# Local attention, top-2 MoE and GLU on one core: three experts begin on the first two batches, the router takes two batches at once, v is loaded once

## The chip, the core and the metric

The kernel runs on one core of one Trainium2 chip. The metric is the device time of one execution in microseconds; lower is better. The engines are TensorE (PE, with its weight load PEld), VectorE (DVE), ScalarE (ACT), GpSimd (POOL) and SyncE (SP). SP issues most transfers from memory, POOL the indirect ones.

## The reference

Three blocks follow one another; all is computed from float32 values.

```python
# attention: q, k, v are [4 batches, 8 heads, 576, 64]
mask_plain = (rel >= 0) & (rel < 32)                      # heads 0 to 3
mask_dil = (rel >= 0) & (rel < 128) & (rel % 4 == 0)      # heads 4 to 7
attn = softmax(where(mask, q @ k.T / 8, -1e9)) @ v
x = attn.transpose(0, 2, 1, 3).reshape(2304, 512)
# mixture of experts: 8 experts of 512 x 1024 x 512, two per row
noisy = x @ w_gate + log1p(exp(x @ w_noise)) * noise
top2 = two largest of noisy; weights = softmax over the two
out[row] += weight * (relu(x[row] @ w1[e]) @ w2[e])       # for both experts of a row
# gated linear unit, 512 x 1536 x 512
out = (silu(x @ w_gate2) * (x @ w_val)) @ w_out
```

## The kernel before

Every engine runs its instructions in the order in which the program writes them, so the place of a line in the Python loops is its place in the engine's queue. Waits between engines are found from the data.

**Attention** has 36 units: a batch has 9, of two blocks of 64 queries each (plain heads, one mixed unit, dilated heads). Because masks are local, a block needs 96 keys. Loop step i does the scores of unit i+1 (`at_S`, L194 puts in the mask, L201 the product), its maximum (DVE), then for unit i−1 the product with v (`at_AV`) and the norm (DVE, which sends the rows to the table `zd` in memory), for unit i−2 the transposes into `xTb`, and for unit i the transposes of the probabilities. v of a batch and head type is a tile of 96 partitions x 4 heads x 9 blocks x 65; neighbouring blocks share 32 rows, which memory holds twice.

**The router** is a generator, `routing`: logits, top two, the row's rank within its expert, and from that a slot number. Products of one-hot matrices (`ob` for the place within 128, `oa` for the column) turn slot numbers into the index table `inva`. It runs in four passes (`groups`, 4 or 5 blocks of 128 rows each, one per batch); three lie in attention, started at i = 11, 20 and 29, and the last in the MoE. `go(n)` and `pump_on(n)` in other code take n pieces of the generator, so each piece is a DVE instruction between those of the host code.

**The MoE** gives an expert up to 640 rows (CAP). A segment is an expert with a range of its slots, and has 8 steps (one per 128 columns of the hidden layer): load 512 KB of weights (`load_raw`, five steps ahead), split them (`split`: high part `whi` on ACT, remainder `wlo` on DVE, L173 and L175; two steps ahead), the hidden layer `moe_h` (three products per chunk, L657), relu into high part and remainder (`hhi` on ACT, `hlo` on DVE, L669 and L670), the output product `moe_y` of the step before (L696). Rows of x are gathered by POOL (`gather_x`, L591) during the segment before, turned (on PE, or in DVE's 32 x 32 transposes, L603, for the segments in DVE_SEGS) and split (`parts`, L616 and L618). Segments: experts 0 and 1 start with slots 0 to 255, which the first two batches fill; then their slots 256 to 639; experts 2 to 6 whole; expert 7 in two parts: 88 steps, of which 0 to 15 are 256 wide, 16 to 31 are 384, 32 to 71 are 640.

**The conversion of the GLU weights** rides on MoE steps named in the list CVS: `cv_tick` takes apart 8-byte numbers with three ACT and seven DVE instructions (L783 to L791) on 512 KB, behind the step's other DVE work. The seven instructions of a load come three ticks later. From step 32 on, five steps in six have a tick.

**The GLU** (72 steps, L1046 and L1070) runs on PE to the end.

`late_consts` casts constants that come with `ccon`. The part under `tc.If` is for experts with over 640 rows, which these inputs do not have.

Of the kernel before, what the change touches and what calls it, by code (L numbers as in the profile page):

```python
# [25 lines left out]
CAP = 640  # L26
EARLY = 256
# [13 lines left out]
def attn_moe_glu_kernel(ctx, tc, qT, kT, vB, cst, wgn, noise, wm, wz, out):  # L41
# [33 lines left out]
    idx = keep.tile([128, NA * E], I32, name="idx")  # L75
# [12 lines left out]
    def load_qkv(b, t):  # L88
# [34 lines left out]
    zs = gp.tile([128, N], F32, name="zs")  # L123
# [12 lines left out]
    V.tensor_copy(maskb.rearrange("p a k -> p (a k)"), zs[:, 0:C_END - C_MASK])  # L136
# [32 lines left out]
    def split(i, eng=V):  # L169
# [125 lines left out]
    groups = [(0, 4), (4, 9), (9, 13), (13, 18)]  # L295
    base = gp.tile([128, 5, E], F32, name="base")
    V.memset(base[:, 0, :], 0.0)
    inva = gp.tile([128, NA * E], F32, name="inva")
    idx0 = gp.tile([128, 2, 2], I32, name="idx0")
# [9 lines left out]
    def routing(gi):  # L309
        g0, g1 = groups[gi]  # L310
        n = g1 - g0
# [6 lines left out]
        def s_z(q):  # L318
            z = bank("f")
            for c in range(4):  # L320
                T.matmul(z[c * 32:c * 32 + 32, 0:S // 2], lhsT=wg[:, c, :],
                         rhs=xTb[gi][:, c, q * (S // 2):(q + 1) * (S // 2)], start=True, stop=True,
                         skip_group_check=True)
            o = gi * S + q * (S // 2)
            A.activation(zs[:, o:o + S // 2], z[:, 0:S // 2], AF.Copy)
# [65 lines left out]
        def s_slot():  # L391
            R = X["f"][:, 128:128 + n * E].rearrange("p (g e) -> p g e", g=n)
            tot = X["f"][:, 176:176 + E]
# [5 lines left out]
            if gi == 1:  # L399
                V.tensor_tensor(base[:, 2, :], base[:, 2, :], floor0, op=OP.max)  # L400
# [8 lines left out]
            a1 = tl("a1", [128, 2, n])  # L409
# [4 lines left out]
            ca = tl("ca", [128, 2, n])  # L414
            V.scalar_tensor_tensor(ca, a1, 8.0, X["ii"], op0=OP.mult, op1=OP.add)
            yield
            sb = tl("sb", [128, 2, n])
# [3 lines left out]
        def s_rows():  # L421
            rf = tl("rf", [128, 2, n])
            V.scalar_tensor_tensor(rf, X["ca"], 128.0, X["sb"], op0=OP.mult, op1=OP.add)
            yield
            V.tensor_scalar(rf, rf, 64.0 * 128 + N, None, op0=OP.add)
            yield
            V.tensor_copy(rowi[:, :, g0:g1], rf)
            yield
            ov = tl("ov", [128, n])
            V.tensor_tensor(ov, X["a1"][:, 0, :], X["a1"][:, 1, :], op=OP.max)  # L430
            yield
            V.tensor_scalar(ov, ov, float(CAP // 128), None, op0=OP.is_ge)
# [12 lines left out]
            V.reciprocal(ww[:, 0, g0:g1], sm)
            yield
            V.tensor_tensor(ww[:, 1, g0:g1], X["ex"], ww[:, 0, g0:g1], op=OP.mult)
            yield
            no = tl("no", [128, n])
            V.tensor_scalar(no, ov, -1.0, 1.0, op0=OP.mult, op1=OP.add)  # L450
            yield
            for k in range(2):
                V.tensor_tensor(wm_[:, k, g0:g1], ww[:, k, g0:g1], no, op=OP.mult)
                yield
            V.tensor_tensor(wm_[:, 0, g0:g1], wm_[:, 0, g0:g1], ov, op=OP.add)
            yield

        def onehots(eng, pairs):
            if "ob" not in X:
                tl("ob", [128, 2 * n, 128], F16)  # L460
                tl("oa", [128, 2 * n, NA * E], F16)
            for i, k in pairs:
                eng.tensor_scalar(X["ob"][:, 2 * i + k, :], iotb, X["sb"][:, k, i:i + 1], None,
                                  op0=OP.is_equal)
                yield
                eng.tensor_scalar(X["oa"][:, 2 * i + k, :], iotc, X["ca"][:, k, i:i + 1],
                                  tokid[:, g0 + i:g0 + i + 1], op0=OP.is_equal, op1=OP.mult)
                yield

        pool = [(i, 1) for i in range(n - 2, n)]  # L470
        mine = [(i, k) for i in range(n) for k in range(2) if (i, k) not in pool]
        order = mine + pool

        def s_inv(pairs):
            iv = X["f"][:, 256:256 + NA * E]
            for pr in pairs:
                j = 2 * pr[0] + pr[1]
                T.matmul(iv, lhsT=X["ob"][:, j, :], rhs=X["oa"][:, j, :], start=pr == order[0],
                         stop=pr == order[-1], skip_group_check=True)

        def s_acc():
            iv = X["f"][:, 256:256 + NA * E]
            if gi == 0:
                V.tensor_copy(inva, iv)
                yield
# [3 lines left out]
            if gi == 1:  # L489
                V.tensor_scalar(idx0, inva.rearrange("p (a e) -> p a e", e=E)[:, 0:2, 0:2], float(ID0), None,  # L490
                                op0=OP.add)
                yield
            if gi == 3:
# [3 lines left out]
                V.tensor_reduce(mx, base[:, 4, :], axis=AX, op=OP.max)  # L497
# [5 lines left out]

        LAG = 1 if gi < 3 else 0
        s_z(0)
        yield NEXT
        s_z(1)
        yield NEXT
# [8 lines left out]
        for _ in onehots(G, pool):  # L517
            pass
        h = len(mine) // 2
        yield from onehots(V, mine[:h])  # L520
        yield NEXT
        A.activation(X["ex"], X["ex"], AF.Exp)
        for _ in range(LAG):
            yield
        s_inv(mine[:h])
        yield from onehots(V, mine[h:])
        yield NEXT
        for _ in range(LAG):
            yield
        s_inv(mine[h:] + pool)  # L530
        yield from s_acc()
        if gi == 3:
            yield NEXT
        yield from s_rows()
        if gi == 3:
            V.tensor_copy(row0, rowm[:, :, 0:LOW // 128])
            yield
            V.tensor_copy(w0, wm_[:, :, 0:LOW // 128])
            yield NEXT
            o = X["f"][:, 0:4 * NSLOT].rearrange("p (t k) -> p t k", t=4)  # L540
            regroup(o, inva[:, 0:NSLOT])
            V.tensor_scalar(idx4, o, 4.0, ccon[:, C_PART + 1:C_PART + 2], op0=OP.mult, op1=OP.add)
            yield NEXT
            o = X["f"][:, 160:160 + 16 * NT].rearrange("p (t k) -> p t k", t=4)
            regroup(o, rw.rearrange("p a k t -> p (a k t)"))
            o4 = o.rearrange("p t (a k) -> p t a k", a=2)
            V.tensor_scalar(row4.rearrange("p t k n -> p t (k n)"), o4[:, :, 0, :], 4.0,
                            ccon[:, C_PART:C_PART + 1], op0=OP.mult, op1=OP.add)
            yield
# [639 lines left out]
```

## Time and profile before

| | |
|---|---|
| median of 3 runs | 1062.88 us (1056.6 to 1073.88) |
| profiled execution | 1065.96 us, span 1063.9 us |
| mean granted clock of TensorE in it | 0.984 of full speed |
| attention | 0 to 113.4 us |
| MoE, 16 steps of 256 | 113.4 to 177.2 us |
| MoE, 16 steps of 384 | 177.2 to 252.9 us |
| MoE, 40 steps of 640 | 252.9 to 531.8 us |
| MoE, expert 7 (8 of 384, 8 of 256) | 531.8 to 595.2 us |
| GLU | 595.2 to 1063.9 us |
| busy | PE 1024.8 us (96%), DVE 600.0 (56%), ACT 427.2 (40%), POOL 331.5 (31%) |

The profile shows one execution. Times in rows are microseconds from the span's start. PE's share of busy time is a mean over stages with different limits, so the stages are looked at one by one.

### The profile page before, as it was taken

How to read it: one execution, taken by the hardware profiler on the slowest of the kernel's cores; microseconds unless marked ns; L12 is line 12 of the kernel's file. 1: busy time of each engine (PE TensorE's matmuls, PEld its weight loads, DVE VectorE, ACT ScalarE, POOL GpSimd, SP SyncE). 2: the span in 40 equal slices, each digit the busy share in tenths (PEclk: the TensorE clock that was granted, in tenths of full speed). 3: DMA queues.
4: the chain of work that ended last, by engine and by line, in shares of the span. 5: the costliest groups of instructions: out<-in, count | busy, mean ns of one | idle time of the engine just before them, and what ended most of it. 6: DMA issues, size and time to landing. Idle time of an engine off the chain costs nothing. (4 is left out here: it accounts for less than half of the span.)

```text
span 1063.9 us, 16850 instructions
## 1 busy us (share of the span) xinstructions
PE 1024.8 (96%) x6561; PEld 920.1 (86%) x6562; DVE 600.0 (56%) x1259; ACT 427.2 (40%) x840; POOL 331.5 (31%) x324
## 2 busy tenths in 40 slices
PE   8988988899999999999999999799999999999998
PEld 5776777788999989899989899699999999999997
DVE  3587685468898788897865443134244233343222
ACT  4786543355565555565544322123122122122111
POOL 0023347626343526260001477315126035000000
PEclk8998999999999999999999999899999999999999
DMA  9994355566677777867686586101101101000000
GB/s 252 260 281 148 105 162 179 198 201 187 243 266 254 240 238 242 285 221 238 219 294 223 209 299 228 58 10 40 40 13 43 35 20 40 30 1 1 30 1 30
DMA packets 60980, 161.33 MB, mean 152 GB/s; under 512 B 10048, under 2 KB 17344, under 8 KB 60224
## 3 DMA queue, kind: packets, MB, share of 16 engines
q1 hardware_dynamic: 47904, 120.95, 35.4%
q0 software_dynamic: 12560, 38.82, 11.1%
q8 instruction: 52, 0.85, 0.3%
q10 hardware_dynamic: 432, 0.44, 0.1%
q14 instruction: 32, 0.26, 0.1%
HBM read 121.37 MB, written 38.80 MB: 151 GB/s over the span
## 5 line engine op out<-in xcount | busy, mean ns | idle before, releaser
L591 POOL DMA_INDIRECT xg<-zd,idx x139 | 158.0, 1137 | 168.4 <-DVE xtl L618 127.3
L591 POOL DMA_INDIRECT yg<-zd,row x126 | 122.8, 974 | 200.4 <-DVE yg L844 128.3
L657 PE MATMUL bA<-xth,whi 128*128 128x320 f32 (+2 forms) x452 | 115.9, 314 | 11.9 <-DVE hlo L670 6.1
L657 PE MATMUL bA<-xtl,whi 128*128 128x320 f32 (+2 forms) x452 | 114.9, 312 | 0.2 <-issue 0.2
L657 PE MATMUL bA<-xth,wlo 128*128 128x320 f32 (+2 forms) x452 | 114.6, 311 | 0.0
L1054 DVE TENSOR_TENSOR t<-bB,ex 128x384 f32<-128x384 f32 x36 | 20.1, 558 | 152.6 <-ACT ex L1052 137.8
L669 ACT ACTIVATE hhi<-bA 128x640 fp32r<-128x640 f32 (+2 forms) x73 | 42.4, 581 | 155.7 <-PE bA L657 129.2
L175 DVE TENSOR_TENSOR wlo<-raw,whi 128x1024 fp32r<-128x1024 f32 x80 | 97.2, 1215 | 8.9 <-ACT whi L173 7.7
L657 PEld LDWEIGHTS bA<-xth,whi 128*128 128x128 f32 x452 | 80.6, 190 | 20.8 <-DVE hlo L670 9.2
L173 ACT ACTIVATE whi<-raw 128x1024 fp32r<-128x1024 f32 x88 | 92.7, 1054 | 0.0
L670 DVE SCALAR_TENSOR_TENSOR hlo<-bA,hhi 128x640 fp32r<-128x640 f32 (+2 forms) x73 | 48.9, 669 | 74.8 <-ACT hhi L669 59.1
L657 PEld LDWEIGHTS bA<-xtl,whi 128*128 128x128 f32 x452 | 79.3, 190 | 1.4 <-issue 0.5
L657 PEld LDWEIGHTS bA<-xth,wlo 128*128 128x128 f32 x452 | 79.5, 190 | 0.0
L1052 ACT ACTIVATE ex<-bB 128x384 f32<-128x384 f32 x36 | 17.7, 492 | 151.7 <-PE bB L1046 120.5
L1058 ACT ACTIVATE th<-t 128x384 fp32r<-128x384 f32 x72 | 37.9, 526 | 87.7 <-DVE t L1055 71.8
L1054 DVE TENSOR_TENSOR t<-bA,ex 128x384 f32<-128x384 f32 x36 | 20.1, 558 | 93.3 <-ACT ex L1052 82.3
L1059 DVE TENSOR_TENSOR tl<-t,th 128x384 fp32r<-128x384 f32 x72 | 40.3, 559 | 42.7 <-ACT th L1058 40.9
L1046 PE MATMUL bA<-x2h,wl 128*128 128x384 f32 x288 | 57.7, 340 | 4.6 <-issue 4.6
L1046 PE MATMUL bB<-x2h,wh 128*128 128x384 f32 x288 | 57.3, 341 | 0.0
L1046 PE MATMUL bA<-x2h,wh 128*128 128x384 f32 x288 | 56.5, 338 | 0.3 <-PEq L977 0.3
L1046 PE MATMUL bB<-x2h,wl 128*128 128x384 f32 x288 | 56.4, 337 | 0.0
L1046 PE MATMUL bB<-x2l,wh 128*128 128x384 f32 x288 | 56.3, 337 | 0.0
(233 smaller groups left out, 2353.3 us busy)
## 6 DMA issues: line engine op xcount, KB each, us to landing
raw<-in_wm SPq DMA_DIRECT2D x88, 512.0 KB
r<-in_wz SPq DMA_DIRECT2D x36, 512.0 KB
zd<-y SPq DMA_DIRECT2D x40, 256.0 KB
whd<-cvh SPq DMA_DIRECT2D x36, 256.0 KB
wld<-cvl SPq DMA_DIRECT2D x36, 256.0 KB
wh<-whd POOLq DMA_DIRECT2D x12, 768.0 KB
wl<-wld POOLq DMA_DIRECT2D x12, 768.0 KB
v<-in_vB SPq DMA_DIRECT2D x7, 877.5 KB
```

The lines of the kernel that those rows point to most:

```text
L173: A.activation(whi[i], raw[i], AF.Copy)
L175: eng.tensor_tensor(wlo[i], raw[i], whi[i].bitcast(F32), op=OP.subtract)
L591: G.indirect_dma_start(out=g, out_offset=None, in_=src, in_offset=bass.IndirectOffsetOnAxis(ap=ix, axis=0))
L657: T.matmul(hp[:, q, 0:cw], lhsT=wt[:, ws], rhs=xt[:, c, q * cw:q * cw + cw], start=c == 0 and j == 0, stop=c == 3 and j == 2)
L669: A.activation(a3, hp, AF.Relu)
L670: V.scalar_tensor_tensor(l3, hp, 0.0, a3.bitcast(F32), op0=OP.max, op1=OP.subtract)
L1046: T.matmul(p[:, q, 0:LOW], lhsT=w[:, ws], rhs=x[:, c, :], start=c == 0 and j == 0, stop=c == 3 and j == 2, skip_group_check=True)
L1052: A.activation(ex, p[:, 0, 0:LOW], AF.Sigmoid)
L1054: V.tensor_tensor(t, p[:, 0, 0:LOW], ex, op=OP.mult)
L1058: A.activation(a, t, AF.Copy)
L1059: V.tensor_tensor(l, t, a.bitcast(F32), op=OP.subtract)
```

## The change

Three experts (NE) start with slots 0 to 255 instead of two, so the segments are experts 0, 1, 2 with 256, then the same three with 384, then experts 3 to 6 with 640 and expert 7 in two parts: 96 steps, of which 0 to 23 are 256 wide, 24 to 47 are 384, 48 to 79 are 640. Expert 2's weights are loaded and split twice. The router has two passes of nine blocks: batches 0 and 1 in attention from i = 20, batches 2 and 3 in the MoE, a few instructions per step. Its one-hots are built by wide two-input instructions on DVE. POOL keeps the gathers and loses the splits, its one-hots and the spreading copies `xk` (now on ACT). v is loaded once, on partitions 32 to 95; partitions 0 to 31 are copied from 64 to 95 by DVE. CVS starts eight steps later. Of the early splits, two are left in attention. Loads of constants and early weights move.

```diff
+NE = 3
-            SP.dma_start(v[:, :, a:z, :], vB[b, t, :, :, a:z, :])
+            SP.dma_start(v[32:96, :, a:z, :], vB[b, t, :, :, a:z, :])
+    def before_v(b, t, a, z):
+        v = vt[b, t]
+        if a == 0:
+            V.memset(v[0:32, :, 0, :], 0.0)
+            a = 1
+        V.tensor_copy(v[0:32, :, a:z, :], v[64:96, :, a - 1:z - 1, :])
...
-    segs = [(0, 0, EARLY), (1, 0, EARLY), (0, EARLY, CAP), (1, EARLY, CAP)] \
-        + [(e, 0, CAP) for e in range(2, E - 1)] + [(E - 1, 0, LOW), (E - 1, LOW, CAP)]
+    segs = [(e, 0, EARLY) for e in range(NE)] + [(e, EARLY, CAP) for e in range(NE)] \
+        + [(e, 0, CAP) for e in range(NE, E - 1)] + [(E - 1, 0, LOW), (E - 1, LOW, CAP)]
...
-            eng.tensor_tensor(wlo[i], raw[i], whi[i].bitcast(F32), op=OP.subtract)
+            V.tensor_tensor(wlo[i], raw[i], whi[i].bitcast(F32), op=OP.subtract)
...
-    groups = [(0, 4), (4, 9), (9, 13), (13, 18)]
...
+    def logits_of(b, banks):
+        for q, bk in enumerate(banks):
+            z = bank(bk)
...
+    def routing(gi, banks):
+        n = NT // 2
+        g0, g1 = gi * n, gi * n + n
...
-                eng.tensor_scalar(X["ob"][:, 2 * i + k, :], iotb, X["sb"][:, k, i:i + 1], None,
-                                  op0=OP.is_equal)
-                yield
-                eng.tensor_scalar(X["oa"][:, 2 * i + k, :], iotc, X["ca"][:, k, i:i + 1],
-                                  tokid[:, g0 + i:g0 + i + 1], op0=OP.is_equal, op1=OP.mult)
...
+            for k in range(2):
+                for i in range(0, n, 3):
+                    V.tensor_tensor(ob[:, k, i:i + 3], iotb[:, None, :].to_broadcast([128, 3, 128]),
+                                    sb[:, k, i:i + 3, None].to_broadcast([128, 3, 128]), op=OP.is_equal)
+                    yield
+                    if gi == 0:
+                        yield
+                        yield
+                V.tensor_tensor(oa[:, k], iotc[:, None, :].to_broadcast([128, n, NSLOT]),
+                                ca[:, k, :, None].to_broadcast([128, n, NSLOT]), op=OP.is_equal)
+                yield
+                V.tensor_tensor(oa[:, k], oa[:, k], tokid[:, g0:g1, None].to_broadcast([128, n, NSLOT]),
+                                op=OP.mult)
...
-            if s < 2:
+            if s < NE:
                 gather(g, xd[0:2 * S, :], idx0[:, a, e:e + 1])
...
-            G.tensor_copy(spread(g), by_chunk(rows))
+            A.activation(spread(g), by_chunk(rows), AF.Copy)
...
-    DVE_SEGS = (3, 11)
-    CVS = [17, 20, 23, 26, 29] + [32 + round(1.2 * j) for j in range(3 * NK + CV_LAST - 4)]
+    DVE_SEGS = (NE + 1, len(segs))
+    CVS = [25, 28, 31, 34, 37] + [40 + round(1.2 * j) for j in range(3 * NK + CV_LAST - 4)]
...
         if i > 2:
-            pump_on(3)
+            pump_on(1)
         moe_relu(i)
-        go(5)
+        go(2)
...
-        sp = split(i + 2, G if i < 11 and i % 2 else V) if i >= 2 else iter(())
+        sp = split(i + 2)
...
-    LOADS = (15, 17, 19, 23, 25)
-    SPLITS = (20, 22, 24, 26)
+    LOADS = (15, 17, 28, 33, 34)
+    SPLITS = (21, 23), (31, 33)
+    halves = [split(j) for j in range(2)]
...
-        if i == 2:
+        if i == 7:
             SP.dma_start(ccon[:, 128:C_MASK], cst[:, 128:C_MASK])
...
-            if (i - 11) % 9 == 0:
-                route.append([routing((i - 11) // 9), False])
+            if i in (11, 30):
+                route.append([logits_of((i - 11) // 9, "ff"), False])
+            elif i == 20:
+                route.append([routing(0, "ff"), False])
...
+        if i == 0:
+            before_v(0, 0, 0, 2)
+        elif i == 1:
+            before_v(0, 0, 2, NB)
+            V.tensor_copy(maskf[:, 192:], zs[:, 192:C_END - C_MASK])
+        elif i < NU and i % 9 in (0, 4):
+            before_v(i // 9, i % 9 // 4, 0, NB)
...
-        if i == 6:
+        if i == 12:
             late_consts()
...
-    route.append([routing(3), True])
+    route.append([routing(1, "fe"), True])
```

DVE in the last segment of 384 rows, before (steps 27 to 29, L670 is `hlo`, L603 and L618 the transpose and remainder of gathered rows, L175 the remainder of the weights, L783 to L791 the conversion of GLU weights):

```order
L670 SCALAR_TENSOR_TENSOR hlo<-bB,hhi 128x384
L603 STREAM_TRANSPOSE xg<-xg 128x512
L175 TENSOR_TENSOR wlo<-raw,whi 128x1024
L618 TENSOR_TENSOR xtl<-xg,xth 128x4x128
L670 SCALAR_TENSOR_TENSOR hlo<-bA,hhi 128x384
L603 STREAM_TRANSPOSE xg<-xg 128x512
L175 TENSOR_TENSOR wlo<-raw,whi 128x1024
L618 TENSOR_TENSOR xtl<-xg,xth 128x4x128
L670 SCALAR_TENSOR_TENSOR hlo<-bB,hhi 128x384
```

The same place now (steps 44 and 45, also the last segment of 384 rows; hlo is L675, the transpose L608, wlo L189, xtl L623, the conversion L788 to L796):

```order
L675 SCALAR_TENSOR_TENSOR hlo<-bA,hhi 128x384
L608 STREAM_TRANSPOSE xg<-xg 128x512
L189 TENSOR_TENSOR wlo<-raw,whi 128x1024
L623 TENSOR_TENSOR xtl<-xg,xth 128x4x128
L788 TENSOR_TENSOR cvw<-r,cvw 128x512
L790 TENSOR_SCALAR cvc<-cvw 128x512
L791 TENSOR_SCALAR cvh<-cvw 128x512
L793 SCALAR_TENSOR_TENSOR cvc<-r,cvc 128x512
L794 SCALAR_TENSOR_TENSOR cvh<-cvw,cvh 128x512
L795 TENSOR_SCALAR cvl<-cvh 128x512
L796 SCALAR_TENSOR_TENSOR cvl<-cvc,cvl 128x512
L675 SCALAR_TENSOR_TENSOR hlo<-bB,hhi 128x384
```

In these eight steps before, two had the seven conversion instructions; now seven have them.

POOL's queue before, from its first work in attention to the first MoE segments (L463 and L466 are one-hots, L643 spreads gathered rows):

```order
L463 TENSOR_SCALAR g_ob<-iotb,g_sb 128x128
L466 TENSOR_SCALAR g_oa<-iotc,g_ca,ccon 128x144
L463 TENSOR_SCALAR g_ob<-iotb,g_sb 128x128
L466 TENSOR_SCALAR g_oa<-iotc,g_ca,ccon 128x144
L175 TENSOR_TENSOR wlo<-raw,whi 128x1024 x3
...
L175 TENSOR_TENSOR wlo<-raw,whi 128x1024
L591 DMA xg<-zd,idx_140 128x512 x2
L643 COPY xk<-xg 128x512 x2
```

POOL's queue now, from the same place to the last gather of x:

```order
L596 DMA xg<-zd,idx_145 128x512 x6
L596 DMA xg<-zd,idx 128x512 x3
L596 DMA xg<-zd,idx_86 128x128 x124
```

Only gathers are left of POOL's work before the GLU's loads.

DVE in attention now, where one unit has the one-hots and another also the work in v (L444 compares three blocks at once, L450 and L453 make `oa` of nine, L120 and L122 are `before_v`, L223 the maximum, L287 the norm):

```order
L223 TENSOR_REDUCE nm<-bA 128x4
L450 TENSOR_TENSOR g_oa<-iotc,ca 128x360
L453 TENSOR_TENSOR g_oa<-g_oa,ccon 128x360
...
L444 TENSOR_TENSOR g_ob<-iotb,sb 128x384
L287 TENSOR_TENSOR xs<-bd,rec 128x256
L444 TENSOR_TENSOR g_ob<-iotb,sb 128x384
L120 MEMSET v 32x4x65
L122 COPY v<-v 32x4x520
L223 TENSOR_REDUCE nm<-bB 128x4
```

Before, DVE had two instructions per block and choice there, 128 and 144 wide, and nothing of v.

## Rows read from the trace of the kernel before

**Rows 1.** Busy time by stretch: start:end, length, each engine's us, clock, DMA.

```profile
0.00:113.40 113.40, 100.18 (x1545) 74.97 (x1547) 75.95 (x319) 75.52 (x241) 18.91 (x20) 0.92 0.77 223
113.40:177.20 63.80, 56.06 (x416) 48.39 (x415) 45.20 (x142) 27.76 (x56) 33.94 (x31) 1.00 0.53 167
177.20:252.90 75.70, 70.98 (x333) 62.69 (x334) 45.84 (x66) 35.64 (x53) 39.83 (x37) 0.95 0.60 196
252.90:531.80 278.90, 277.25 (x1556) 251.81 (x1555) 234.75 (x368) 152.20 (x217) 102.78 (x88) 1.00 0.72 239
```

**Rows 2.** Timeline of PE, first products of attention units: start, duration, instruction.

```profile
26.45 0.33 PE L194 MATMUL bB<-maskb,identb 128*128 128x192 bf16 x2
...
28.63 0.33 PE L194 MATMUL bA<-maskb,identb 128*128 128x192 bf16 x2
...
76.64 0.33 PE L194 MATMUL bA<-maskb,identb 128*128 128x192 bf16 x2
...
99.04 0.33 PE L194 MATMUL bB<-maskb,identb 128*128 128x192 bf16 x2
```

**Rows 3.** Timeline of PE, first products of neighbouring MoE steps, 384 and 256 wide.

```profile
236.19 0.33 PE L657 MATMUL bA<-xth,whi 128*128 128x384 f32 x1
...
240.38 0.33 PE L657 MATMUL bB<-xth,whi 128*128 128x384 f32 x1
...
579.48 0.28 PE L657 MATMUL bA<-xth,whi 128*128 128x256 f32 x1
...
582.30 0.28 PE L657 MATMUL bB<-xth,whi 128*128 128x256 f32 x1
```

**Rows 4.** The page's DMA issues: queue, count, KB of each.

```profile
v<-in_vB SPq DMA_DIRECT2D x7, 877.5 KB
```

**Rows 5.** Timelines of PE and DVE in attention; brackets hold the idle time before.

```profile
17.77 0.91 PE L201 MATMUL bA<-k,q 64*64 64x96 f32 x14 [2.14 <-DMA k<-in_kT]
...
31.80 0.23 DVE L145 CAST trib<-ccon 128x128 bf16<-128x128 f32 x1 [2.89 <-DMA ccon<-in_cst]
...
32.22 0.42 DVE L148 COPY sel<-ident 128x512 f32<-128x512 f32 x1
```

**Rows 6.** Timeline of all engines around a split on POOL in attention.

```profile
80.64 0.16 DVE L397 TENSOR_TENSOR base<-bf,base 128x8 f32<-128x8 f32 x1
80.68 2.36 POOL L175 TENSOR_TENSOR wlo<-raw,whi 128x1024 fp32r<-128x1024 f32 x1 [3.73 <-ACT whi L173]
...
80.85 2.21 DVE L400 TENSOR_TENSOR base<-base,ccon 128x8 f32<-128x8 f32 x1
```

**Rows 7.** DVE's groups by line and form: count, busy us, mean ns, idle before.

```profile
L175 DVE TENSOR_TENSOR wlo<-raw,whi 128x1024 fp32r<-128x1024 f32 x80 | 97.2, 1215 | 8.9 <-ACT whi L173 7.7 <-issue 0.9
...
L463 DVE TENSOR_SCALAR g_ob<-iotb,g_sb 128x128 f16<-128x128 bf16 x28 | 12.0, 429 | 0.1
...
L466 DVE TENSOR_SCALAR g_oa<-iotc,g_ca,ccon 128x144 f16<-128x144 bf16 x28 | 8.9, 319 | 0.0
...
L707 DVE COPY y<-bd 128x512 f32<-128x512 f32 x9 | 6.1, 682 | 0.0
```

**Rows 8.** Timeline of DVE, two neighbouring steps of 384, the first with a conversion.

```profile
230.64 0.56 DVE L670 SCALAR_TENSOR_TENSOR hlo<-bA,hhi 128x384 fp32r<-128x384 f32 x1 [2.01 <-ACT hhi L669]
...
231.74 1.18 DVE L175 TENSOR_TENSOR wlo<-raw,whi 128x1024 fp32r<-128x1024 f32 x1
232.85 0.68 DVE L618 TENSOR_TENSOR xtl<-xg,xth 128x512 fp32r<-128x512 f32 x1
233.44 0.69 DVE L783 TENSOR_TENSOR cvw<-r,cvw 128x512 f32<-128x512 f32 x1
...
237.30 0.55 DVE L670 SCALAR_TENSOR_TENSOR hlo<-bB,hhi 128x384 fp32r<-128x384 f32 x1
...
240.09 0.54 DVE L670 SCALAR_TENSOR_TENSOR hlo<-bA,hhi 128x384 fp32r<-128x384 f32 x1
```

**Rows 9.** Timeline of PE, the first product of step 16.

```profile
177.22 0.54 PE L657 MATMUL bA<-xth,whi 128*128 128x384 f32 x1 [2.25 <-issue]
```

More of the change, by code (lines that the diff above doesn't have):

```diff
@@ L316, in tl @@
             return X[nm]
[L318 to L325, printed above, removed]
+        ca, sb, a1, ex = ca_[:, :, g0:g1], sb_[:, :, g0:g1], a1_[:, :, g0:g1], ex_[:, g0:g1]
         def s_logits():
@@ L470, in routing, with s_inv @@
[L470 to L479, printed above, removed]
+        def s_inv():
+            iv = X["f"][:, 256:256 + NSLOT]
+            for k in range(2):
+                for i in range(n):
+                    T.matmul(iv, lhsT=X["ob"][:, k, i, :], rhs=X["oa"][:, k, i, :], start=k + i == 0,
+                             stop=k + i == n, skip_group_check=True)
@@ L502, in s_acc, with s_rows @@
                 yield
[L504 to L508, printed above, removed]
+        def s_rows():
+            rf = tl("rf", [128, 2, NT])
+            V.scalar_tensor_tensor(rf, ca_, 128.0, sb_, op0=OP.mult, op1=OP.add)
+            yield
+            V.tensor_scalar(rf, rf, 64.0 * 128 + N, None, op0=OP.add)
+            yield
+            V.tensor_copy(rowi, rf)
+            yield
+            ov = tl("ov", [128, NT])
+            V.tensor_tensor(ov, a1_[:, 0, :], a1_[:, 1, :], op=OP.max)
+            yield
+            V.tensor_scalar(ov, ov, float(CAP // 128), None, op0=OP.is_ge)
+            yield
+            for k in range(2):
+                dt = tl("dt", [128, NT])
+                V.scalar_tensor_tensor(dt, tokid, float(ID0), rf[:, k, :], op0=OP.add, op1=OP.subtract)
+                yield
+                V.tensor_tensor(dt, dt, ov, op=OP.mult)
+                yield
+                V.tensor_tensor(rowm[:, k], rf[:, k, :], dt, op=OP.add)
+                yield
+            sm = tl("sm", [128, NT])
+            V.tensor_scalar(sm, ex_, 1.0, 1e-9, op0=OP.add, op1=OP.add)
+            yield
+            V.reciprocal(ww[:, 0, :], sm)
+            yield
+            V.tensor_tensor(ww[:, 1, :], ex_, ww[:, 0, :], op=OP.mult)
+            yield
+            no = tl("no", [128, NT])
+            V.tensor_scalar(no, ov, -1.0, 1.0, op0=OP.mult, op1=OP.add)
+            yield
+            for k in range(2):
+                V.tensor_tensor(wm_[:, k], ww[:, k], no, op=OP.mult)
+                yield
+            V.tensor_tensor(wm_[:, 0], wm_[:, 0], ov, op=OP.add)
+            yield
+        yield from logits_of(2 * gi + 1, banks)
         s_logits()
@@ L516, in routing @@
         yield from s_slot()
[L517 to L520, printed above, removed]
+        yield from s_onehots()
         yield NEXT
[L522 to L526, printed above, removed]
         yield NEXT
-        for _ in range(LAG):
-            yield
-        s_inv(mine[h:] + pool)
+        s_inv()
         yield from s_acc()
-        if gi == 3:
-            yield NEXT
@@ new lines, in routing @@
+        yield NEXT
+        A.activation(ex_, ex_, AF.Exp)
+        o = X["f"][:, 0:4 * NSLOT].rearrange("p (t k) -> p t k", t=4)
+        regroup(o, inva)
+        yield from s_rows()
+        V.tensor_copy(row0, rowm[:, :, 0:LOW // 128])
+        yield
+        V.tensor_copy(w0, wm_[:, :, 0:LOW // 128])
+        yield
+        V.tensor_scalar(idx4, o, 4.0, ccon[:, C_PART + 1:C_PART + 2], op0=OP.mult, op1=OP.add)
+        yield NEXT
+        o = X["f"][:, 160:160 + 16 * NT].rearrange("p (t k) -> p t k", t=4)
@@ L960, in attn_moe_glu_kernel @@
             gather_x(0, 1)
+        for part in SPLITS:
+            if i in part:
+                next(halves[part.index(i)], None)
     pump_on()
@@ L1154 @@
     kT = halves(kp)
-    vp = pad(order(v))
-    vb = np.stack([vp[:, :, :, j * 64:j * 64 + 96] for j in range(NB)], axis=3)
+    vb = order(v).reshape(B, 2, 4, NB, 64, D)
     vb = np.concatenate([vb, np.ones(vb.shape[:-1] + (1,), vb.dtype)], axis=-1)
```

166 lines of the change are left out of this document (70 added, 96 removed).

## The prediction

> **What bounds the kernel now.** I read the stages first. The table by stretches [rows 1] shows PE busy for 100.18 of 113.40 us in attention, 56.06 of 63.80 in the sixteen MoE steps 256 rows wide, 70.98 of 75.70 in the sixteen that are 384 wide, and 277.25 of 278.90 in the forty that are 640 wide. So from 252.90 on PE is the bound, and an edit counts there only if it changes PE's own work. Before that, 13 us of attention and 12 us of the early MoE are PE waiting, and that is all that a rearrangement can win. DVE is the second engine: 234.75 of 278.90 in the wide steps, 45.84 of 75.70 in the steps of 384.
>
> Next come the floors. An attention unit with nothing in the way goes from one mask product to the next in 28.63 − 26.45 = 2.18 us, and the five units from 76.64 to 99.04 take 22.4 [rows 2]. A step of 384 takes 240.38 − 236.19 = 4.19 us, one of 256 takes 582.30 − 579.48 = 2.82 [rows 3], one of 640 takes 278.90 / 40 = 6.97 [rows 1]. The 32 early steps thus need 16 × 2.82 + 16 × 4.19 = 112.2 and take 63.80 + 75.70 = 139.5: 27.3 over their floor.
>
> **Attention.** (a) v comes on 64 partitions: 585 KB for the 877.5 KB of [rows 4], 292.5 KB less (about 300,000 bytes) ahead of the k on which PE waits for 2.14 us at 17.77 [rows 5]. At the stretch's 223 GB/s [rows 1] that is 1.3 us; the second part of the mask table, now between the loads, takes some back. Ends 0 and −2.1; I take −1.1.
>
> (b) The constants are issued five units later and used six units later, so DVE's wait of 2.89 us for ccon [rows 5] ends long before it is needed: −2.9 (end: −1.5, if PE's queue had hidden half).
>
> (c) The five slow units from 76.64 [rows 2] are 22.4 − 5 × 2.18 = 11.5 over pace. POOL's wlo from 80.68 to 83.04 lies over a DVE operation of eight elements that takes 2.21 us where its neighbour takes 0.16 [rows 6]; this is a hold, and another of the kind is in these units. Beside them lie the 28 pairs of one-hots of 429 + 319 ns on DVE [rows 7], and the row arithmetic of two passes. The change takes POOL's splits and one-hots away altogether, and builds the one-hots in ten wide operations per pass. What stays, the router's products for nine blocks at once and the units that bring its scores, I put at 4.8, a little over two units' pace; no row prices it apart. So 11.5 − 4.8: −6.7 (ends −9 and −3).
>
> (d) The copies inside v, 2080 elements on each of 32 partitions, are on DVE, seven of them behind the first unit. DVE copies 512 elements in 0.42 and casts 128 in 0.23 [rows 5], a slope of 0.5 ns an element: 0.17 + 1.04 = 1.2 us, with the memset 1.4. A unit leaves DVE 2.18 × (1 − 75.95 / 113.40) = 0.72 us, so each overhangs by 0.7, of which PE, one unit ahead of DVE, should feel less than half: +2. The dear end is the copy out of PSUM at 682 ns for 512 [rows 7], 1.33 ns an element: 2.8 us each.
>
> (e) Two wlo splits of 1.2 us [rows 7] come to DVE in units 31 and 33, and ACT gets the spreading copies of the first gathered rows: +2 (ends 0 and +4). With −0.3 for a shorter mask cast ahead of the first unit, attention comes to −1.1 − 2.9 − 6.7 + 2 + 2 − 0.3 = **−7** (ends −12 and −2).
>
> [...]
>
> **Early MoE, steps 0 to 39 after against 0 to 31 before.** The three wlo that POOL did in steps of 256 each held DVE, as in [rows 6], by about 2.1; with them gone some −5 of the 6.3 should show, since DVE was late there (PE idle 7.7 us [rows 1]). Against it stand the transposes of a third expert's rows and more router products on PE, which I put at one step of 256, +2.8; and the second routing pass, now over all of steps 3 to 21 with about three operations a step, whose six comparisons of 384 and four of 360 elements stand on DVE between hlo and the splits: +2. Taking 0.8 for the gathers that no longer queue behind POOL's work: **−1** (ends −6 and +5). The late completions behind the rest of the 27.3 I carry over.
>
> **The extra steps.** There are 24 + 24 + 32 steps in place of 16 + 16 + 40: 8 × (2.82 + 4.19 − 6.97) = **+0.3**. The eight additional loads of 512 KB lie under PE.
>
> **The term that decides.** The conversion of the GLU weights (seven DVE operations a tick) becomes dense at step 40 in place of step 32. Before, step 32 is the first of 640; now the 640s begin at step 48. So steps 40 to 47, 384 wide, carry seven ticks, and five of them also the transposes and lows of the next segment. Such a step has been seen: from hlo at 230.64 through transpose, wlo, xtl at 232.85 and the tick from 233.44 to the next hlo at 237.30 is 6.66 us on DVE, against 2.79 without the tick (237.30 to 240.09) [rows 8]. A step with tick and no transpose takes hlo 0.5, wlo 1.1 (231.74 to 232.85) and tick 3.86 (233.44 to 237.30), 5.4; with the copy of y, 6.0. By the written order the eight steps need 6.0 + 5.4 + 6.66 + 2.79 + 3 × 6.66 + 5.4 = 46.2 us on DVE. PE needs 8 × 4.19 = 33.5. Each hlo releases the next y, so DVE is the bound there, less about 2 us that the double buffers take up: the single burst of [rows 8] came with PE still at its floor [rows 3]. 46.2 − 33.5 − 1.9 = **+10.8** (ends +7, if two ticks slide into the first 640 step, and +15).
>
> **Sum.** −7 − 1 + 0.3 + 10.8 = +3.1. The profiled execution took 1065.96 us, 3.1 above the median of the runs shown, 1062.88; against that median the forecast is **1066 us**, no change that counts (about 2% is what a measurement of this kernel can tell). Nothing of the GLU stage, 468.7 us on PE, changes.
>
> **Rivals.** *Faster, 1048.* The crowded steps are absorbed, because POOL's work no longer meets DVE's and PE gets further ahead: that term is +3, attention is at its good end −12, the early MoE −6: −14.7 against the median. For it: one burst was already absorbed without loss. Against it: seven in eight steps is a mean, not a burst, and the sum of the DVE rows alone exceeds PE's time. Chance 0.22.
>
> *Slow copies inside v, 1076.* If a copy between partition groups runs at the PSUM price, seven times 1.5 us more fall on a DVE that has 0.72 to spare: +10. For it: no row shows such a shift of partitions. Chance 0.12.
>
> *Slower, 1087.* [...] Chance 0.11. [...]
>
> **How the numbers follow.** The forecast's own case has 0.55 and spans 1055 to 1077. The range, **1045 to 1081**, takes in the two rivals beside it, and leaves out the slower case and the tails of the others, about 0.2. Under 1041.6 lie only the best end of the faster rival and a gain of which I know nothing, 0.08; over 1084.1 the slower one and little else, 0.10; between, 0.82.
>
> **What the changed profile will show.** Attention ends at 105 to 108 us and not 113.4; no DVE operation of a few elements takes over 1 us; the wait for ccon is gone and that for k is about 1. The copies in v take about 1.2 us. Steps 40 to 47 last about 5.5 us each, PE's idle time there ends with hlo, DVE is over 0.9 busy, and the granted clock is 1.00. From the first 640 step on the steps take 6.9 to 7.0. Wrong would be: steps 40 to 47 near 4.3 us (then DVE's rows overlap more than I count), or losses in steps 3 to 21 larger than before (then the routing at three operations a step sits in front of hlo).

## The result, and the profile after

The changed kernel takes 1073.55 us (median of 4, 1071.84 to 1075.64) against 1062.99 for the kernel before (median of 4, 1056.6 to 1073.88): **1.0115 times, interval 1.0072 to 1.0158**, 1.2% slower. The forecast was 1066 in a range of 1045 to 1081.

In this first comparison the traces of both kernels show long pauses that no later trace shows; in later runs, on four chips, the kernel before takes 1039 to 1040 us. So the parts are compared below between two traces taken on one of these chips, where the changed kernel's ratio is 1.0100 (1.0077 to 1.0122). There one execution of each kernel took far longer (1990 and 5037 us) and is left out of the ratios. Busy time by stretch on that chip, the kernel before first: attention; steps 0 to 31, up to the first step of 640, in two pieces; then, after a row left out for the rest of the MoE, the GLU with step 87 (columns as in [rows 1]).

```profile
0.00:108.59 108.59, 96.42 (x1546) 72.24 (x1547) 75.35 (x319) 75.17 (x241) 18.86 (x20) 0.97 0.78 233
108.59:170.71 62.12, 57.03 (x416) 49.66 (x416) 45.62 (x142) 28.22 (x56) 32.03 (x29) 0.97 0.51 162
170.71:237.17 66.46, 66.46 (x335) 59.98 (x333) 45.55 (x66) 35.20 (x53) 42.40 (x39) 1.00 0.70 231
...
571.47:1037.10 465.63, 460.14 (x2409) 429.30 (x2407) 164.95 (x322) 110.10 (x238) 127.02 (x140) 1.00 0.18 63
```

The changed kernel there: attention; steps 0 to 23 (256 wide); 24 to 39; 40 to 49, of which 48 and 49 are 640 wide; the rest of the MoE is left out; the GLU with step 95.

```profile
0.00:109.11 109.11, 95.81 (x1529) 72.45 (x1531) 73.71 (x238) 73.42 (x235) 6.43 (x10) 0.94 0.65 211
109.11:195.89 86.78, 80.01 (x586) 70.33 (x584) 57.98 (x128) 46.46 (x83) 19.22 (x17) 1.00 0.55 184
195.89:262.21 66.32, 66.32 (x334) 60.04 (x333) 43.83 (x62) 34.04 (x51) 33.99 (x31) 1.00 0.66 221
262.21:320.99 58.78, 49.36 (x241) 42.85 (x240) 54.57 (x89) 34.87 (x53) 21.61 (x20) 0.97 0.75 256
...
585.77:1046.50 460.73, 455.98 (x2409) 425.77 (x2407) 164.72 (x322) 110.11 (x238) 126.68 (x140) 1.00 0.19 64
```

The spans differ by 1046.5 − 1037.1 = 9.4 us, and these rows split it. Attention: +0.5. Early MoE: 86.78 + 66.32 = 153.1 for 40 steps whose floor is 134.7, so 18.4 over; before, 62.12 + 66.46 = 128.6 against 112.2, 16.4 over: +2.0. Steps 40 to 49: 58.78, where the same ten steps take 46.0 when nothing waits (experiment 7): +12.8, with DVE busy 54.57 of 58.78. The last row: −4.9, of which the GLU itself is −4.2 (458.8 and 454.7 us) and step 87 or 95 the other 0.7 (6.79 and 6.08). The rest, with the eight extra steps in it, is −1.0.

What answers to [rows 8] is in the first trace of the changed kernel: DVE in steps 44 to 46 and PE's wait in step 46 (L675 is `hlo`, L788 the conversion's first, L701 the output product).

```profile
300.02 0.55 DVE L675 SCALAR_TENSOR_TENSOR hlo<-bA,hhi 128x384 fp32r<-128x384 f32 x1
...
306.66 0.55 DVE L675 SCALAR_TENSOR_TENSOR hlo<-bB,hhi 128x384 fp32r<-128x384 f32 x1
...
309.46 0.68 DVE L788 TENSOR_TENSOR cvw<-r,cvw 128x512 f32<-128x512 f32 x1
...
313.31 0.54 DVE L675 SCALAR_TENSOR_TENSOR hlo<-bA,hhi 128x384 fp32r<-128x384 f32 x1
```

```profile
311.32 0.40 PE L701 MATMUL bc<-wlo,hhi 128*128 128x512 f32 x1
313.91 0.50 PE L701 MATMUL bc<-whi,hlo 128*128 128x512 f32 x1 [2.19 <-issue]
```

One hlo follows the other after 6.64 and 6.65 us, as 6.66 in [rows 8], and PE's product with hlo starts only when hlo is done at 313.85. In the second trace, that of the tables above, PE idles 58.78 − 49.36 = 9.4 us in steps 40 to 49, and every one of its waits there ends with an hlo; the longest, between steps 48 and 49:

```profile
312.50 0.90 PE L662 MATMUL bA<-xth,whi 128*128 128x320 f32 x2 [3.74 <-DVE hlo L675]
```

In the steps of 256 PE idles 86.78 − 80.01 = 6.8 us, and 62.12 − 57.03 = 5.1 before. What it waits for has changed (the kernel before, then the changed kernel in step 3, both from the traces of the tables):

```profile
119.19 0.66 PE L608 MATMUL be<-ident,xk 128*128 128x128 f32 x4 [0.78 <-POOL xk L643]
...
137.45 0.39 PE L657 MATMUL bA<-xth,whi 128*128 128x256 f32 x1 [1.71 <-DVE hlo L670]
```

```profile
125.34 0.66 PE L613 MATMUL be<-ident,xk 128*128 128x128 f32 x4 [1.32 <-ACT xk L648]
```

Before, 3.6 of the 5.1 are two waits for hlo, and 0.8 is the one for a spreading copy, which POOL made. Now 5.9 of the 6.8 are seven waits for the spreading copies, which ACT makes, and none ends with hlo.

Attention stayed level because gains were given back where the prediction had priced low, most of all at two places. The first is unit 28 (the loop's step 28), where the copy in v stands behind the one-hots on DVE (first trace of the changed kernel, DVE, then PE):

```profile
82.94 0.55 DVE L444 TENSOR_TENSOR g_ob<-iotb,sb 128x384 f16<-128x384 bf16 x1
83.48 0.28 DVE L120 MEMSET v<- 32x260 f32 x1
83.78 1.23 DVE L122 COPY v<-v 32x2080 f32<-32x2080 f32 x1
```

```profile
83.85 0.45 PE L252 MATMUL be<-v,pT 96*64 96x65 f32 x2 [2.69 <-issue]
85.07 1.13 PE L252 MATMUL be<-v,pT 96*64 96x65 f32 x14 [0.77 <-DVE v L122]
```

The copy itself takes 1.23 us, as estimated. PE waits 3.5 us around it, and the granted clock is 0.51 from 83.3 to 90.2 (1.00 from 76.0 to 83.3 and from 90.2 to 97.0). Other copies cost PE less, but are not hidden; this is the first of batch 1:

```profile
33.32 0.68 PE L252 MATMUL be<-v,pT 96*64 96x65 f32 x14 [0.62 <-DVE v L122]
```

From the first product of unit 11 to that of unit 12 it is 3.1 us, where a unit takes 2.2. The second place is units 33 and 34, where PE waits for ACT's spreading copies:

```profile
103.45 0.66 PE L613 MATMUL bB<-ident,xk 128*128 128x128 f32 x4 [1.46 <-ACT xk L648]
...
108.36 0.66 PE L613 MATMUL bA<-ident,xk 128*128 128x128 f32 x4 [2.18 <-ACT xk L648]
```

```profile
101.86 1.01 ACT L234 ACTIVATE p<-bA,nb 128x96 f32<-128x96 f32 x4
102.76 0.64 ACT L648 ACTIVATE xk<-xg 128x512 f32<-128x512 f32 x1
```

ACT takes the copy only after the four exponentials written ahead of it, though POOL issued the gathers of the first rows at 91.0 to 93.4.

### The profile page after: what moved, and what is told of

The parts are those of the page before. It is cut to its first block, busy times and chain, and to the rows that moved or that the text cites. A ratio compares the mean times of both kernels' runs of the same rounds, so it can differ in the third digit from the quotient of the medians.

```text
span 1070.0 us, 16778 instructions
## 1 busy us (share of the span) xinstructions
PE 1020.4 (95%) x6569; PEld 915.2 (86%) x6570; DVE 604.5 (56%) x1159; ACT 438.5 (41%) x858; POOL 286.2 (27%) x287
## 5 line engine op out<-in xcount | busy, mean ns | idle before, releaser
L596 POOL DMA_INDIRECT xg<-zd,idx x133 | 150.0, 1128 | 339.8 <-DVE xtl L623 111.9
L189 DVE TENSOR_TENSOR wlo<-raw,whi 128x1024 fp32r<-128x1024 f32 x96 | 116.8, 1216 | 15.0 <-ACT whi L187 12.7
L662 PE MATMUL bA<-xth,whi 128*128 128x320 f32 (+2 forms) x428 | 113.3, 314 | 4.8 <-DVE hlo L675 4.8
L662 PE MATMUL bA<-xtl,whi 128*128 128x320 f32 (+2 forms) x428 | 112.3, 311 | 0.0
L662 PE MATMUL bA<-xth,wlo 128*128 128x320 f32 (+2 forms) x428 | 112.1, 311 | 0.0
L187 ACT ACTIVATE whi<-raw 128x1024 fp32r<-128x1024 f32 x96 | 101.0, 1053 | 0.0
L674 ACT ACTIVATE hhi<-bA 128x640 fp32r<-128x640 f32 (+2 forms) x75 | 41.1, 548 | 141.8 <-PE bA L662 124.3
L662 PEld LDWEIGHTS bA<-xth,whi 128*128 128x128 f32 x428 | 77.6, 191 | 11.4 <-DVE hlo L675 7.6
L675 DVE SCALAR_TENSOR_TENSOR hlo<-bA,hhi 128x640 fp32r<-128x640 f32 (+2 forms) x75 | 47.1, 629 | 64.6 <-ACT hhi L674 54.7
L662 PEld LDWEIGHTS bA<-xtl,whi 128*128 128x128 f32 x428 | 76.4, 191 | 1.4
L662 PEld LDWEIGHTS bA<-xth,wlo 128*128 128x128 f32 x428 | 76.3, 191 | 0.0
L1085 ACT ACTIVATE ex<-bA 128x384 f32<-128x384 f32 x36 | 17.7, 491 | 96.8 <-PE bA L1079 90.3
```

What stands on the lines that cost most here:

```text
L189: V.tensor_tensor(wlo[i], raw[i], whi[i].bitcast(F32), op=OP.subtract)
L596: G.indirect_dma_start(out=g, out_offset=None, in_=src, in_offset=bass.IndirectOffsetOnAxis(ap=ix, axis=0))
L662: T.matmul(hp[:, q, 0:cw], lhsT=wt[:, ws], rhs=xt[:, c, q * cw:q * cw + cw], start=c == 0 and j == 0, stop=c == 3 and j == 2)
L674: A.activation(a3, hp, AF.Relu)
L675: V.scalar_tensor_tensor(l3, hp, 0.0, a3.bitcast(F32), op0=OP.max, op1=OP.subtract)
L1085: A.activation(ex, p[:, 0, 0:LOW], AF.Sigmoid)
```

## The experiments

Ratios are against the kernel before on the same chip. Where one is set beside the changed kernel, that is its 1.0100 of experiment 5, taken on another chip than experiments 1 to 4; on theirs, experiment 3, an edit without effect, has 1.0096.

**1. Dense conversion only from step 48.**

```diff
-CVS = [25, 28, 31, 34, 37] + [40 + round(1.2 * j) ...]
+CVS = list(range(22, 47, 3)) + [48 + round(1.2 * j) ...]
```

> The changed kernel with the conversion of the GLU weights sparse (one step in three, from step 22) up to step 46 and dense only from step 48, the first of 640. Theory A (DVE rows in steps 40 to 47 exceed PE's time): steps 40 to 49, 58.7 us in the changed kernel against a floor of 47.4, come back to within 2 us of the floor, and the time falls by about 10, to 1063. Rival (the loss there comes from the long row of gathers on POOL and the lower clock): the stretch keeps 5 us or more of its loss and the time falls by less than 5.

Measured: 1.0028 (1.0014 to 1.0042), 0.7% under the changed kernel. Steps 40 to 49 in its trace:

```profile
263.53:311.17 47.64, 46.27 (x242) 41.79 (x240) 39.82 (x63) 28.82 (x44) 22.04 (x20) 1.00 0.67 222
```

47.64 in place of 58.78, with as many gathers on POOL and the clock at 1.00: theory A holds, and the rival falls. Some 6 of the 11 us were lost again in steps 32, 75, 85 and 94, where PE waits for DVE (0.8, 1.3 and 1.3 us for hlo, 1.6 for a spreading copy of the GLU's rows).

**2. The spreading copies earlier in ACT's queue.**

```diff
+        if i + 1 in FIRST_X:
+            early[i + 1] = trans_x(0, FIRST_X.index(i + 1), into(i + 2))
+            next(early[i + 1])
         if i + 1 < NU:
             at_exp(i + 1)
...
+        if s < NE - 1:
+            next(tx, None)
         moe_relu(i)
```

> The changed kernel with ACT's spreading copy of gathered rows put earlier in ACT's queue: before the four exponentials of the unit ahead in attention, before the relu in steps 0 to 15. Theory B (PE waits because the copy stands behind other ACT work): PE's waits for the copy at units 33 and 34 (1.46 and 2.18 us) and in steps 2, 3 and 20 (about 1 each) go, and the time falls by 5 to 7, to 1067. Rival (the rows come late, not the copy): the waits move to the gathers, ACT is held by them, and the time falls by less than 2 or rises.

Measured: 1.0023 (1.0010 to 1.0036), 0.8% less; step 24 begins 6.1 us earlier than in experiment 1, whose program is the same up to there but for the first tick, in step 22. The waits at units 33 and 34 and in steps 2 and 3:

```profile
98.06 0.66 PE L613 MATMUL bB<-ident,xk 128*128 128x128 f32 x4 [0.55 <-ACT xk L648]
101.87 0.66 PE L613 MATMUL bA<-ident,xk 128*128 128x128 f32 x4 [1.07 <-ACT xk L648]
115.66 0.60 PE L613 MATMUL be<-ident,xk 128*128 128x128 f32 x4
121.25 0.66 PE L613 MATMUL be<-ident,xk 128*128 128x128 f32 x4 [1.05 <-ACT xk L648]
```

They shrink (by 0.9, 1.1, 1.0 and 0.3 against the changed kernel on another of these chips) and steps 10 and 11 give 1.8 more: theory B, but the waits at the two units and in step 3 do not go altogether, and the edit does not reach those of steps 20 to 22 (0.55 each).

**3. Gathers paced by ACT's work.**

```diff
+                if s != NE - 1:
+                    G.tensor_copy(held[0:96], hh_[i - 1][0:96, 0:1].bitcast(F32) if i else spT[NU - 1][:, 0:1])
                 gather_x(s + 1, b0 + fg)
```

> The changed kernel with one element copied by POOL from a tile that ACT writes in the step before, ahead of each step's gathers, so that POOL cannot run ahead with its gathers. Theory C (PE is starved while POOL issues gathers without a pause: 94.3 to 97.2 us in attention, 196.6 to 203.1 in step 22): these two stalls go, 3 and 6 us, with the lower clock that follows each, and the time falls by 6 to 12, to about 1064. Rival (the stalls have another cause and only coincide): they stay, and the later gathers cost up to 5 more.

Measured: 1.0096 (1.0070 to 1.0123), no change. But on this chip the unpaced kernels have no such stalls either: step 22 takes 4.0 us in all of them. So nothing follows on theory C; where the pauses of the first comparison come from stays open.

**4. v on 96 partitions, no copies.**

```diff
-            SP.dma_start(v[32:96, :, a:z, :], vB[b, t, :, :, a:z, :])
+            SP.dma_start(v[:, :, a:z, :], vB[b, t, :, :, a:z, :])
```

> The changed kernel with v loaded on 96 partitions as before and no copies in it. Theory D (the copy stands behind seven one-hots at unit 28 and costs PE 3.5 us there and the lower clock after it, elsewhere it is hidden): attention is shorter by 4 to 6 after unit 27 and k comes about 1 later, the time falls by 3 to 5. Rival (the load saved is worth more than the copies cost): no change or slower by 1 to 3.

Measured: 1.0048 (1.0025 to 1.0072), 0.5% less. Attention ends at 105.48 and not 109.11. PE waits for k again,

```profile
18.10 0.55 PE L215 MATMUL bA<-k,q 64*64 64x96 f32 x14 [1.84 <-DMA k<-in_kT]
```

and unit 5 starts at 20.8 in place of 17.3, 3.5 later; the end is 3.6 earlier all the same, so from unit 5 on the copies cost 7 us of attention. Theory D, and more than it said. Its "elsewhere it is hidden" is wrong: at five other copies the unit is longer by 0.9 to 1.3 us than here, at unit 28 by 3.7. That makes near 9; some 1.5 of it is set off by a wait for `wg` that the changed kernel does not have:

```profile
39.23 0.69 PE L329 MATMUL bf<-xTb,wg 128*32 128x288 f32 x8 [1.54 <-DMA wg<-in_wgn]
```

**5 and 6. The changed kernel and the kernel before, once more, for two traces on one chip.**

> The changed kernel once more, beside the others of this call. Theory A, B and D together (crowded steps, copies behind ACT's work, copies in v): on a chip where the long stalls of steps 22 and 23 and of the GLU do not occur, the change still costs 0.6 to 0.8% against the kernel before, steps 40 to 49 take 58 to 59 us and PE waits for the spreading copies at units 33 and 34. Rival (the loss of the first comparison was that chip's stalls): within 0.3% of the kernel before.

> The kernel before, for its trace on the same chip: if the stalls with late products (steps 16 to 18, 23, 32 to 33 and 15 us in the GLU) belong to the chip and not to the kernel, they are gone here and its span is 20 to 25 us shorter than in the first trace. If they belong to the kernel, they stand in both.

Measured: 1.0100 (1.0077 to 1.0122), and 1.0009 (0.9992 to 1.0025) for the kernel before against itself. The loss is the change's own, and larger than the 0.6 to 0.8% expected. The pauses do not belong to the kernels: in the first trace steps 16 to 18 of the kernel before took 19.4 us and here 12.0, and a GLU step of 15.2 us is back at 6.3.

**7. Three edits together:** the copies as in 2, v loaded a second time for batches 1 to 3, and other ticks.

```diff
+            if b:
+                SP.dma_start(v[0:32, :, 1:NB, :], vB[b, t, 32:64, :, 0:NB - 1, :])
+                G.memset(v[0:32, :, 0, :], 0.0)
...
+CVS = [18, 20, 22, 25, 28, 30, 34, 37, 43, 46] + list(range(48, 80))
```

> The changed kernel with three edits: conversion ticks sparse up to step 46 and in every step from 48 to 79, the spreading copies earlier in ACT's queue, and for batches 1 to 3 the first 32 partitions of v loaded a second time in place of the copy (its zero block by POOL). Theory: the three costs add up, so steps 40 to 49 come to 48 to 50 us, the waits at units 33 and 34 go, attention ends at 101 to 103, and the time is 1.2 to 1.8% under the changed kernel and 0.6 to 1.2% under the kernel before. Rival (they are covers of one another, PE waits for the next late thing): less than 0.6% under the changed kernel.

Measured: **0.9882 (0.9864 to 0.9899)**, 2.2% under the changed kernel. Attention ends at 100.1, steps 40 to 49 take 46.0. The costs add up: 0.7, 0.8 and 0.5% alone, 2.2% together. The waits at units 33 and 34 do not go, though (1.66 and 0.86 us).

**8. The kernel before, POOL's splits on DVE.**

```diff
-        sp = split(i + 2, G if i < 11 and i % 2 else V) if i >= 2 else iter(())
+        sp = split(i + 2, V) if i >= 2 else iter(())
...
-            list(split(SPLITS.index(i), G))
+            list(split(SPLITS.index(i), V))
```

> The kernel before with POOL's eight splits on DVE and nothing else changed. My prediction's step (POOL's splits hold DVE's two-input work for about 2.1 us each, and DVE needs 1.2 for one itself): 3 to 8 us faster, no short DVE instruction over 1 us at units 26 to 30 and in steps 5 to 10. Rival (the holds lie where DVE has time): within 2 us, or slower by up to 3 as DVE takes on 8 x 1.2 us.

Measured: 0.9967 (0.9949 to 0.9985), 3 us faster. In the kernel before, the holds of [rows 6] stand on this chip too:

```profile
77.46 2.20 DVE L400 TENSOR_TENSOR base<-base,ccon 128x8 f32<-128x8 f32 x1
...
133.10 2.33 DVE L368 TENSOR_TENSOR g_M<-g_cc,g_ii 128x40 f32<-128x40 f32 x1
...
140.60 2.42 DVE L410 TENSOR_SCALAR g_a<-g_rr 128x10 f32<-128x10 f32 x1
```

With the splits on DVE they are gone, and steps 0 to 31 take 124.3 in place of 128.6: −4.2. Attention ends 3.1 later, of which 1.3 is there at unit 20, before the first split. So in attention the holds gone gave nothing that the four splits of 1.2 us on DVE did not take back.

**9 and 12. The kernel before, the GLU's weights at another place in memory.**

```diff
+    shift = ctx.enter_context(tc.tile_pool(name="shift", bufs=1))
+    pad = shift.tile([128, 8], F32, name="pad")
+    V.memset(pad, 0.0)
     wp = ctx.enter_context(tc.tile_pool(name="wp", bufs=1))
```

(Experiment 12 has 104 in place of 8.)

> The kernel before with 32 bytes per partition allocated ahead of the GLU weights of blocks 2 to 11, so that they begin at a multiple of 64 bytes as in the changed kernel; nothing else changes but one clear of these 32 bytes. Theory E (the GLU is 4.9 us shorter in the changed kernel, 6.25 against 6.32 us a step, only because these tiles lie elsewhere): the GLU's steps take 6.25 and the time falls by 4 to 5. Rival (the order of the work around the GLU does it, or it is another boundary than 64 bytes): the steps keep 6.32 and the time stays within 1.

> The kernel before with 416 bytes per partition ahead of the GLU weights of blocks 2 to 11 in place of 32. These tiles then begin 256 bytes past a multiple of 512, as in the changed kernel; they began 352 past one before, and 384 past one in the run with 32 bytes (6.32 and 6.35 us a step). Theory E, with the place counted in 256 or 512 bytes: 6.25 us a step, and the time falls by 4 to 5. Rival (what the changed kernel does ahead of the GLU shortens its steps): 6.31 or more, and the time stays within 2.

Measured: 1.0016 (0.9998 to 1.0034) with 32 bytes, 0.9947 (0.9926 to 0.9969) with 416. The first products of two neighbouring GLU steps, in the kernel before, then with 416 bytes:

```profile
645.62 1.57 PE L1046 MATMUL bB<-x2h,wh 128*128 128x384 f32 x8
...
651.95 1.55 PE L1046 MATMUL bA<-x2h,wh 128*128 128x384 f32 x8
```

```profile
642.97 1.55 PE L1049 MATMUL bB<-x2h,wh 128*128 128x384 f32 x8
...
649.23 1.55 PE L1049 MATMUL bA<-x2h,wh 128*128 128x384 f32 x8
```

6.33 us a step become 6.26 without any instruction of the GLU being changed; with 32 bytes it is 6.35. The kernel before holds a control of its own: two of every twelve steps use the weights of blocks 0 and 1, which lie elsewhere and are not moved, and these take 6.25 to 6.27 in all of these runs (the step from 651.95 is the first of such a pair). In the changed kernel, where every step takes 6.25, other small tiles are held ahead of the weights, and counted from the program's tiles (no trace shows an address) they begin 96 bytes earlier, which but for 512 bytes is where 416 bytes put them. So the 4.2 us in its GLU come from the place of the tiles: 60 steps at 0.07. The 0.7 in the step before the GLU is not explained by it. That 64 bytes matter, as I first expected, is wrong.

**10. The combined kernel with its first ticks moved.**

```diff
+CVS = [19, 22, 24, 27, 30, 33, 37, 39, 43, 46] + list(range(48, 80))
```

> The combined kernel with the first conversion ticks at steps 19, 22, 24, 27, 30, 33, 37, 39, 43 and 46, so that the first one with ACT work is no longer in step 22. Theory: steps 22 and 23, 10.5 us in the combined kernel and 6.9 in the changed one, come back to 7 and the time falls by 2 to 4. Rival (POOL's and the router's work there): no change.

Measured: **0.9861 (0.9841 to 0.9882)**, the fastest version, 1.4% under the kernel before and 2.4% under the changed one. Steps 22 and 23 take 6.9 us, as expected, not 10.4. Attention, steps 0 to 23 and steps 40 to 49:

```profile
0.00:99.08 99.08, 89.54 (x1529) 67.81 (x1531) 64.46 (x226) 73.33 (x235) 8.92 (x16) 1.00 0.78 249
99.08:182.57 83.49, 79.57 (x584) 70.33 (x584) 57.83 (x129) 46.37 (x83) 19.22 (x17) 1.00 0.59 198
...
248.92:295.98 47.06, 46.29 (x242) 41.82 (x240) 39.82 (x63) 28.47 (x44) 22.03 (x20) 1.00 0.66 224
```

**11. The same with two early experts.**

```diff
-NE = 3
+NE = 2
...
+CVS = [17, 18, 20, 21, 23, 26, 29] + [32 + j for j in range(35)]
-            pump_on(1)
+            pump_on(2)
...
-        go(2)
+        go(4)
```

> The combined kernel with two experts beginning early instead of three, the conversion in every step from 32 on, and the router's second pass taken at twice the pace, since its result is needed eight steps earlier. Theory (the third expert buys room for the router's second pass and costs 0.6 us of PE): the router's DVE work and PE products crowd into steps 3 to 12, which lose 3 to 8 more, the time rises by 2 to 7. Rival (three early experts are what makes the change slow): it falls by 2 or more.

Measured: 0.9876 (0.9858 to 0.9893), 2.2 us more by the medians; the intervals overlap. The third early expert is not what made the change slow, and it is worth little: with two, steps 3 to 12 take 40.0 us in place of 36.0, as the theory has it, and part of that comes back elsewhere.

## Why the prediction came out as it did

The range held the time. The forecast of no change that counts stood beside a measured 1.2% more; as the sum goes, +3 was forecast and +9.4 measured between the two undisturbed traces. That the time came so near is in part luck: attention and the early MoE missed by 10.5 together, and the GLU's −4.9, of which the prediction knew nothing, took half of it back.

- **The term that decides** was right in place, cause and size. By the written order DVE needs 46.2 us for steps 40 to 47; from the hlo of step 40 to that of step 48 it takes 46.6 (278.71 to 325.33 in the first trace). The forecast of +10.8 measured +12.8, and experiment 1 takes 11 of it away. Only its shape was off: the loss is not even over eight steps; up to step 40 there is none (4.18 us in the first trace), and it comes out in 41, 44 and 46 to 49. Steps 40 to 47 lose 6.2 of the 12.8 (5.0 us each, not 5.5), and 6.5 fall on steps 48 and 49, which were to take 6.9 to 7.0 and take 10.6 and 8.5. The slower rival's +21 (1087 for 1066), a lower clock in each of the eight steps, is a term that no run shows. A lower clock came in one piece of 3.4 us (from 312.3, as step 49 begins, with a mean of 0.97 over steps 40 to 49; in two in the first trace, 0.51 over the 3.4 us from 315.4 and 0.50 over those from 325.7). In the kernel before it is 0.54 from 177.2 to 180.0, after the wait of [rows 9]. At 0.5 the one piece is worth at most 1.7 of the 2 us above the forecast.
- **Attention is the step that failed: −7 forecast, +0.5 measured.** (a) was mis-sized to the good side: 3.2 to 3.5 in place of 1.1, because the lower clock that followed the wait goes with it (in the first traces 0.50 from 17.0 to 20.0 before, 1.00 from 17.0 to 27.0 now; experiment 4). (b) gave some 1.4 between the undisturbed traces. (c) gave 2.5 in place of 6.7 (five units in 18.4 us, before 20.9), because the dearest copy of (d), 3.7 us, fell into the same units. The copies together, priced at +2, cost 7. The price of one copy was right to 0.03 us. What failed is "PE should feel less than half" of 0.7 us: at five of the copies PE loses about 1, and 3.7 at unit 28. There it needs that v at once, and the copy is queued behind eight one-hot operations (six of L444, L450 and L453, from 77.85 on), not the seven of experiment 4's text. (e), +2, measured +4.3 at units 33 to 35, since ACT's queue and not its busy time decides when the spreading copy runs (experiment 2 gives back 2.8 in attention, the rest of its 6 in the steps).
- **Early MoE: −1 forecast, +2.0 measured.** The holds were worth 4.2 (experiment 8), 5 forecast. (POOL makes four splits there, not three; three of them hold DVE.) What went against it is a term that the prediction does not have: it moves the spreading copies to ACT and prices that in attention alone, while in steps 2 to 22 PE waits 5.9 us for them, 0.8 before. Step 3 shows this beside the router: it takes 7.8 us and not 4.7, with 1.3 for the spreading copy and 2.1 for the router's products for nine blocks. Larger losses in steps 3 to 21, named as a sign of being wrong, came (14.1 us over their floor, 12.4 before), but not for the reason named with it: no wait there ends with hlo.
- **The load of v on 64 partitions**, which the kernel before does not have, is quicker than its load on 96: the packets of the first whole v lie between 11.78 and 14.59 us, 2.8 us, in the second trace of the changed kernel, where they took 5.1 (14.71 to 19.84) in that of the kernel before, other loads running beside them in both; in the first traces it is 2.6 (11.85 to 14.42) and 6.9 (14.17 to 21.10). The 2.3 between the second traces are more than the 1.3 that (a) took from the bytes. The k that PE waited 1.5 to 2.1 us for comes in time with v on partitions 32 to 95 (unit 5 at 17.3, against 20.8 with 96 partitions).
- **Nothing of the GLU changes** was wrong by −4.2, for a reason that no row of queues shows (experiment 12).
- The rival of slow copies in v falls by its price (1.23 us, not 2.8), though the copies cost most of its +10 at the quick price. That of absorbed crowding falls too.

## What to carry to other kernels

When a schedule is shifted by a count of steps, ask which width the steps at the new place have: the same dense work on a second engine is free in steps of 6.94 us and stretches steps of 4.19 to as much as 6.6 (hlo to hlo, steps 44 to 46). An operation that a bound engine waits for is priced by what is queued ahead of it, not by its own duration: the v copy of 1.23 us cost 3.5 at one place and about 1 at five others, and the spreading copy of 0.64 cost 2.2. When work moves to another engine, price it at every place where it stands: the spreading copies cost more in the MoE than in attention. After a change of small tiles, compare the pace of an untouched loop before explaining the total.

## What was not expected of the hardware

- The same 24 products of 384 columns and 9 of 512 take 6.25, 6.32 or 6.35 us a step, by where their weights begin on each partition: moved by 416 bytes, as in the kernel before, or moved by 32. Eight products take 1.57 us in the slower place (the step at 645.62) and 1.55 in the faster; over the 60 steps concerned it is 4 us. Which boundary decides was not tried beyond these three places.
- In the first comparison both kernels ran 2% slower than on the four chips of the later runs, with long pauses of PE, some beside long rows of gathers on POOL. In the changed kernel's first trace steps 22 and 23 take 14.27 us with POOL busy for 10.34, in its second 6.92 with 5.40:

```profile
193.57:207.84 14.27, 7.76 (x43) 6.89 (x42) 3.31 (x5) 3.04 (x5) 10.34 (x11) 0.76 0.39 118
```

```profile
188.97:195.89 6.92, 6.37 (x44) 5.51 (x42) 3.73 (x6) 4.24 (x7) 5.40 (x6) 1.00 0.59 185
```

The gathers are there in both; why PE stops in one alone, and whether it is the chip, stays open.
